# QK-norm attention and a squared-ReLU feed-forward on one core: output weights loaded in parts, odd pairs' squares in a free weight form, a scale and the last rows moved

## The chip, the cores and the metric

The kernel runs on one core of a Trainium2 chip. The time is the device time of one execution in microseconds (us). Three executions of the kernel before took 1393.12, 1393.48 and 1394.81 us; the median is 1393.48.

The engines of a core work side by side, each on its own instructions in order: TensorE (PE in the profile, PEld for its weight loads), VectorE (DVE), ScalarE (ACT), GpSimd (POOL) and SyncE (SP), which issues nearly all DMAs here. They wait for each other on semaphores.

## The reference

Attention over 8 batches, 12 heads, 448 positions and 64 channels, with q and k divided by their root mean square and multiplied by a gain; then a feed-forward with a squared ReLU on the 3584 tokens of 768 channels.

```python
def rmsnorm(x, g):
    rms = np.sqrt(np.mean(x * x, axis=-1, keepdims=True) + 1e-06)
    return x / rms * g
q_n, k_n = (rmsnorm(q, g_q), rmsnorm(k, g_k))
scores = scale * np.matmul(q_n, k_n.transpose(0, 1, 3, 2))
scores = scores - np.max(scores, axis=-1, keepdims=True)
attn = np.exp(scores)
attn = attn / (np.sum(attn, axis=-1, keepdims=True) + 1e-09)
x = np.matmul(attn, v)      # (B,H,S,D) -> (B*S, H*D)
h = np.maximum(x @ w_in, 0.0)
out = h * h @ w_out
```

Everything is float32.

## The kernel before

**Attention.** It goes by pairs of heads: 6 pairs to a batch, 48 in all, numbered i. Of each pair q and k are squared (`Rows.square`, L181, on ScalarE, into a tile `squares`), summed over channels by VectorE (`Rows.add`, L194 and L197), raised to the power -1/2 by GpSimd (`Rows.power`, L204), and q is scaled (`Rows.scale`, L219). From the third batch on q goes out to DRAM and comes back in blocks (`store_q`, `load_blocks`), VectorE transposes the blocks (`turn_blocks`, L367), and ScalarE multiplies the turned q by the gain (L369). The scores are matmuls (`score`, L435, L446), the exponentials ScalarE activations that write the tile `wT` (`weigh`, L454), the products with v matmuls (`attend`, L536, L550, L571), and the sums of the weights are added up by GpSimd (L473) and summed over partitions by matmuls with ones (L602, L611). `take_sums` puts them into a tile `inverse`, which `invert` or `invert_both` turns into reciprocals and GpSimd multiplies onto the result (L630 for an even pair, L690 for an odd one). `inverse` and `squares` are two names for one buffer: both have the tag "squares" with `bufs=1`, so each waits until the other has been used up. An even pair's squares have 512 columns, an odd one's 384, since the last 64 rows of two pairs are kept with the even one.

**Feed-forward.** It goes by units u of two batches, four units in all. The matrix products use fewer multiplications than the plain ones: products P1 to P7 of sums and differences of quarter blocks, in the first unit one level of it (L986), in units 1 to 3 two levels for the product with w_in (`deep_products`, L1042). Each unit has four blocks. In a block 28 steps of the deep products fill the tiles `hid`, then the generator `second_products` multiplies them by w_out (L1251, 384 columns each; one product of the source is 4 MATMULs in the trace). The output weights stand in DRAM as 8 forms of 128 x 384 ("11", "12", "21", "22", "T1" to "T4", in this order); a tile `out_sb` holds the 8 forms, two such tiles make a block, and there are two buffers for them. P1 reads form 11, P2 21, P3 22, P4 T4, P5 T1, P6 T2 and P7 T3. Form 12 is read only where the 64 last rows of a batch are multiplied (`multiply_rest`, L1165), which is in units 0 and 3; units 1 and 2 (`KEPT`) put those rows by in DRAM, and the last unit works them off as a row block `NT` of its own (`extra`).

**The order.** The source lays down each engine's order by hand. `run` steps the feed-forward's generators and after each step calls `follow_loads`, which counts down `later` (closures with a number of steps to wait), then takes some tasks of the attention: `tasks` and `pool_tasks`, the deques into which `prepare`, `additions` and the visits put their closures. A visit to a pair stands between the steps: its matmuls are one run on TensorE. `drain` ends a unit: it takes the rest of the stream and then all tasks. `visit_whole` is the visit to a pair from i = 25 on; it attends to pair i - 1 and scores pair i in turns.

The loads of the next output weights are put by at the end of a block (L902 issues them):

```python
later.append([4, lambda: [load_out(n + 2) for n in ns]])
```

Pieces of the deep weights (`load_piece`, L892) go into a ring `in_sb` of 42 places, some four pieces ahead of their use. All of these loads, and those of q, k and v, are in SP's one queue in the order of the source. The results of a row block are added up in `accs` by VectorE (L1345, L1272) or written first by ScalarE (L1341, L1266), and stored in the last block (`store`, L1350).

Of the kernel before, what the change touches and what calls it, by code (L numbers as in the profile page):

```python
# [14 lines left out]
F32 = mybir.dt.float32  # L15
# [8 lines left out]
P = 128  # L24
# [201 lines left out]
def program(ctx, tc, rows, v, g, wide, ones, moe_w_in, moe_w_out, out, shift):  # L226
# [50 lines left out]
    def whole(i):  # L277
        return i > 2 * 2 * NPAIR
# [85 lines left out]
    def turn_blocks(i, x):  # L364
        ensure("blocks", i, x)
        dst = att.tile([P, S], F32, name="qT" if x == 0 else "kT")
        nc.vector.transpose(dst, room_for_blocks(i, x))  # L367
        if x == 0:
            nc.scalar.mul(dst, dst, g)  # L369
        turned[i, x] = dst  # L370

    def load_v(i):
        b, c = pairs[i]
# [321 lines left out]

    def leave(i):
        b, c = pairs[i]
        for x in range(2):
            del turned[i, x]
        del values[i]  # L700
        if b == 1:
            begin_forms(c)
        elif b > 1:
            settle(b, c)
# [191 lines left out]
        side, place = divmod((n * 10 + PLACES[m]) % (2 * SIDE_OF_RING), SIDE_OF_RING)  # L896
        return ring[side][:, place]

    def load_out(n):
        if NF // 2 <= n < B // 2 * NF // 2:  # L900
            out_sb[n] = new_out()
            nc.sync.dma_start(out_sb[n], out_forms[n % (NF // 2)])  # L902

    roles = [banks[n] for n in (7, 6, 5)]

    def turn_roles(*order):
# [9 lines left out]
    FIRST_ORDER = ["P1", "P5", "P2", "P6", "P3", "P4", "P7"]  # L916
    FIRST_OF_BLOCK = ["P1", "rest0", "P5", "P4", "P6", "P2", "rest1", "P3", "P7"]
    SECOND_ORDER = ["P1", "P2", "P5", "P6", "P4", "P3", "P7"]
    SPLIT_ORDER = [
# [285 lines left out]
    def second_products(u, blk, hid, sums_, accs):  # L1205
# [20 lines left out]
                yield len(some) * COST_OUT  # L1226
            turn_roles(2, 1, 0)

        def store_rows(tt, e):
# [5 lines left out]
            store(accs[-1] if tt is None else accs_of(tt)[e], parts)  # L1235

        def accs_of(tt):
            return extra["accs"] if tt == NT else accs[2 * tt : 2 * tt + 2]
# [53 lines left out]
        if split:  # L1292
            places = [*roles, banks[1], banks[2]]
            for name, tt, n in SPLIT_ORDER:
# [9 lines left out]
                if tt:  # L1304
                    store_some(name)
                yield COST_OUT
        for tt in range(0 if split else NT + final):
            order = SECOND_ORDER if tt or not u else FIRST_OF_BLOCK
            for name in order:
                if name.startswith("rest"):  # L1310
                    a = int(name[-1])
                    multiply_rest(
                        u, blk, hid, banks[2:0:-1], PARTS_BY_ROW[2 * a : 2 * a + 2],
                        accs[-1] if a else None,
                    )
# [5 lines left out]
                product(tt, name, ps, nc.scalar if order is SECOND_ORDER else nc.vector)  # L1321
                if name == "P1" and order is FIRST_OF_BLOCK:
                    yield from sums_behind_first()
                    continue
                if order is not FIRST_OF_BLOCK:
                    store_some(name)
                yield COST_OUT
            turn_roles(2, 0, 1)
        while to_store and blk == NBLK - 1:
            some = to_store.popleft()  # L1330
            if final:
                store_rows(*some)
            else:
                later.append([2, lambda some=some: store_rows(*some)])
        for n in ns:
            del out_sb[n]
        later.append([4, lambda: [load_out(n + 2) for n in ns]])

    def add_to(acc, ps, first=False, engine=nc.scalar):
        if first and engine is nc.scalar:  # L1340
# [2 lines left out]
            nc.vector.tensor_copy(out=acc, in_=ps)  # L1343
        else:
            nc.vector.tensor_tensor(out=acc, in0=acc, in1=ps, op=ALU.add)  # L1345
    def store(acc, parts):

        at = 0
        for b, row, n in parts:
            nc.sync.dma_start(out[ds(b * S + row, n), :], acc[at : at + n, :])  # L1350
            at += n


# [181 lines left out]
    def follow_loads():  # L1535

        for some in to_load:
            some[0] -= 1
        while to_load and to_load[0][0] <= 0:
            load_weights(to_load.popleft()[1])  # L1540
        for some in later:
            some[0] -= 1
        while later and later[0][0] <= 0:
            later.popleft()[1]()

# [106 lines left out]
    def square(i, x, room, engine=None):  # L1652
        if i <= last:
            ensure("qk", i)
            ensure("qk", i - i % 2)
            rows.square(i, x, room[:, 0 : 4 * P], engine)

    def normalize(i, x):

# [67 lines left out]
    def visit_among(i, n):  # L1727
# [21 lines left out]
        elif whole(i + 1):  # L1749
            prepare(i + 3)  # L1750

    def prepare(i, gaps=0):

        if i > last:
            return
        room = []
        tasks.extend([gap] * gaps)
        tasks.append(
            lambda: room.append(io.tile([P, 4 * P], F32, name="squares", tag="squares", bufs=1))
        )  # L1760
# [11 lines left out]
    def visit_whole(i):  # L1772
        late = [some for some in tasks if getattr(some, "args", None) == (i,)]
        for some in late:
            tasks.remove(some)
        run_all()
        if shift:
            attend_all(i - 1)
            if i <= last:
                weigh_slots(i, 1)  # L1780
        else:
            if i % 2 == 0:
                both_denominators(i - 2)
            for n in range(NJ):
                attend(i - 1, (n,))
                forget(i - 1, (n,))
                if i <= last:
                    score(i, n)
                    weigh(i, n)
                while n == 1 and i % 2 == 0 and late:  # L1790
                    late.pop(0)()
            if i % 2:
                attend(i - 1, (NJ,))
                forget(i - 1, (NJ,))
            join_halves(i - 1)
            if i % 2 == 0:
                tasks.append(lambda: invert_both(i - 2))
                if i <= last:
                    score(i, NJ)
                    weigh(i, NJ)  # L1800
            if i <= last:
                additions(i)
        tasks.extendleft(reversed(late))
# [15 lines left out]
    with tc.manual_schedule(engines=ENGINES):  # L1819
# [8 lines left out]
        for i in range(len(pairs) + 1):  # L1828
            for n in range(1 if whole(i) else VISITS):
                at = i * VISITS + n - VISITS - unit  # L1830
                if at < 0:
                    visit_alone(i, n)
                    continue
                u, x = divmod(at, unit)
                if x == 0:
                    u, x = u - 1, unit
                run(place(u, x - (1 if whole(i - 1) else 0.5)))
                if i < last:
                    if whole(i) and not shift:
# [58 lines left out]
```

## Time and profile before

| what | value |
|---|---|
| median of three runs | 1393.48 us |
| the profiled execution | 1394.38 us |
| its span (first to last instruction of the program) | 1392.6 us |
| granted TensorE clock, mean | 0.998 |
| output weight loads | 24 of 1536 KB, 9.9 us to landing (6.6 to 12.9) |
| deep weight loads of 384 KB | 64, 4.2 us to landing |
| odd pairs' squares, one | 0.52 us |
| scale of a turned q, one | 0.67 us |
| last matmul ends, span ends | 1385.1, 1392.6 us |

The profile has one execution. "Busy" is the time in which an engine works, as a share of the span; an instruction that waits isn't counted. A line of the timeline has the start and the length in us, the engine, the source line, the operation, what it writes and reads, its shape and the number of instructions merged; in brackets stands how long the engine was idle before and for what. A line of the windows view has for each stretch the time of PE, PEld, DVE, ACT and POOL with instruction counts, then the granted TensorE clock, the DMA share and GB/s. Unit 0 of the feed-forward runs from about 128 to 487 us, unit 1 from 496 to 806, unit 2 to 1102, unit 3 to the end; attention goes on beside them until 1087 us.

### The profile page before, as it was taken

The numbers are of one execution on the slowest core, as the hardware profiler recorded it, in microseconds if no ns is written. First come the engines' busy times: TensorE is split into PE (matmuls) and PEld (weight loads), VectorE is DVE, ScalarE is ACT, GpSimd is POOL, SyncE is SP. The second block draws the span as 40 slices with busy tenths as digits, with TensorE's granted clock in tenths as the row PEclk, the third lists the DMA queues.
The fourth block names the chain that finished last, engine by engine and source line by source line (L and its number), as shares of the span: only waits on it lengthen the run. The fifth ranks groups of instructions, "written<-read, shape, count | busy, mean of one in ns | idle before, by whom it ended". The sixth has DMA issues, their size and how long they took to land.

```text
span 1392.6 us, 19474 instructions
## 1 busy us (share of the span) xinstructions
PE 1363.3 (98%) x6320; PEld 845.7 (61%) x6320; DVE 807.2 (58%) x1635; ACT 608.3 (44%) x1118; POOL 789.6 (57%) x794
## 2 busy tenths in 40 slices
PE   7999999999999999999999999999999999999997
PEld 3333444444444466676758586676768677868684
DVE  4786545867758755555556755455546642445444
ACT  6885477757666244353434244442434032202020
POOL 5668664746656868576667877566745630303030
PEclk9999999999999999999999999999999999999999
DMA  5566746968769875664739475755527442424223
GB/s 147 149 168 169 203 117 159 264 179 219 233 155 284 231 215 162 187 173 141 204 86 279 140 225 149 211 153 176 146 86 239 142 165 103 135 90 149 78 90 100
DMA packets 385588, 233.36 MB, mean 168 GB/s; under 512 B 272452, under 2 KB 354244, under 8 KB 381380
## 3 DMA queue, kind: packets, MB, share of 16 engines
q1 hardware_dynamic: 385184, 231.95, 57.7%
q8 instruction: 52, 0.85, 0.3%
q14 instruction: 60, 0.49, 0.1%
q10 hardware_dynamic: 292, 0.07, 0.0%
HBM read 174.59 MB, written 57.34 MB: 167 GB/s over the span
## 4 chain that ended last, share of the span: by engine, by line
PE 81%; POOL 4%; DVE 4%; DMA 3%; issue 3%; SPq 2%; ACT 2%; POOLq 0%; ACTq 0%; DVEq 0%
PE bank L1251 30%; PE bank L1042 20%; PE bank L986 8%; PE bank L446 5%; PE bank L536 5%; PE bank L550 4%; PE bank L435 4%; PE bank L1165 2%; POOL sum L473 2%; PE bank L585 1%; DMA qk<-in_k_dram 1%; PE bank L611 1%; SPq L326 1%; SPq L318 1%; PE bank L571 1%
## 5 line engine op out<-in xcount | busy, mean ns | idle before, releaser
L1042 PE MATMUL bank<-xT,in_sb 128*128 128x224 f32 x1344 | 289.3, 354 | 2.9 <-ACT part L1031 2.3
L1251 PE MATMUL bank<-out_sb,hid 128*128 128x384 f32 x768 | 272.5, 488 | 2.2 <-POOL out_sb L1514 1.4
L1345 DVE TENSOR_TENSOR acc<-acc,bank 128x384 f32<-128x384 f32 x312 | 166.6, 548 | 164.6 <-PE bank L1251 138.1
L1042 PEld LDWEIGHTS bank<-xT,in_sb 128*128 128x128 f32 x1344 | 252.6, 190 | 15.0 <-ACT wT L454 5.6
L454 ACT ACTIVATE wT<-bank,rr 128x448 f32<-128x448 f32 x288 | 163.5, 631 | 155.1 <-PE bank L435 92.7
L1251 PE MATMUL bank<-out_sb,sums 128*128 128x384 f32 x576 | 207.2, 490 | 1.3 <-DVE acc L1345 0.9
L1251 PEld LDWEIGHTS bank<-out_sb,hid 128*128 128x128 f32 x768 | 144.7, 190 | 104.5 <-issue 5.6
L204 POOL TENSOR_TENSOR rr<-ms,minus_half 128x8 f32<-128x8 f32 (+1 forms) x96 | 146.0, 1521 | 73.7 <-DVE ms L197 63.8
L1251 PEld LDWEIGHTS bank<-out_sb,sums 128*128 128x128 f32 x576 | 107.7, 190 | 86.3 <-issue 4.3
L1027 DVE TENSOR_TENSOR hid<-hid,bank 128x224 f32<-128x224 f32 x312 | 111.0, 383 | 83.9 <-PE bank L1042 79.1
L986 PE MATMUL bank<-xT,in_sb 128*128 128x448 f32 x336 | 131.9, 546 | 0.1
L473 POOL TENSOR_TENSOR sum<-sum,wT 128x448 f32<-128x448 f32 (+1 forms) x96 | 110.6, 1173 | 8.1 <-ACT wT L454 6.6
L986 PEld LDWEIGHTS bank<-xT,in_sb 128*128 128x128 f32 x336 | 62.1, 190 | 69.0 <-issue 60.2
L446 PE MATMUL bank<-qT,kT 64*128 64x448 f32 (+1 forms) x492 | 100.5, 571 | 1.9 <-DVE qT L409 1.1
L473 POOL TENSOR_TENSOR sum<-wT 128x448 f32<-128x448 f32 x48 | 55.8, 1183 | 69.8 <-ACT wT L454 69.8
L1099 ACT ACTIVATE hid<-hid 128x448 f32<-128x448 f32 x96 | 55.0, 573 | 66.7 <-DVE hid L1027 48.5
L435 PE MATMUL bank<-qT,kT 64*64 64x448 f32 x552 | 77.0, 547 | 1.9 <-ACT wT L454 1.9
L1042 PE MATMUL bank<-more,in_sb 128*128 128x224 f32 x288 | 76.2, 357 | 1.4 <-DVE hid L1037 1.4
L550 PE MATMUL bank<-wT,vt 64*64 64x448 f32 x576 | 74.3, 548 | 0.0
L1039 ACT COPY hid<-bank 128x448 f32<-128x448 f32 x24 | 12.8, 532 | 137.3 <-PE bank L1042 137.3
L369 ACT ACTIVATE qT<-qT,g 128x448 f32<-128x448 f32 x34 | 22.6, 665 | 113.7 <-DVE qT L367 113.7
L446 PEld LDWEIGHTS bank<-qT,kT 64*128 64x128 f32 (+1 forms) x492 | 34.9, 166 | 60.4 <-issue 36.8
(140 smaller groups left out, 2059.1 us busy)
## 6 DMA issues: line engine op xcount, KB each, us to landing
out_sb<-out_forms SPq DMA_DIRECT2D x24, 1536.0 KB, 9.9
in_sb<-in_deep SPq DMA_DIRECT2D x64, 384.0 KB, 4.2
in_sb<-in_deep SPq DMA_DIRECT2D x80, 256.0 KB, 4.1
words<-in_moe_w_in_dram SPq DMA_DIRECT2D x32, 384.0 KB, 3.8
words<-in_moe_w_out_dram SPq DMA_DIRECT2D x32, 384.0 KB, 3.6
out_forms<-out_sb SPq DMA_DIRECT2D x8, 1536.0 KB, 7.5
qk<-in_q_dram SPq DMA_DIRECT2D x96, 96.0 KB, 2.6
qk<-in_k_dram SPq DMA_DIRECT2D x96, 96.0 KB, 2.7
```

Of the source, the lines that this page charges most:

```text
L204: self.nc.gpsimd.tensor_tensor(out=self.rr[i][:, x, 0 : self.count(i)], in0=ms, in1=self.minus_half.to_broadcast(list(ms.shape)), op=ALU.pow,)
L435: nc.tensor.matmul(sc[ds(half * D, D)], lhsT=turned[i, 1][ds(e * D, D), ds(m * P + half * D, D)], rhs=turned[i, 0][ds(e * D, D), :], start ...
L446: nc.tensor.matmul(sc[some], lhsT=turned[p, 1][r, keys], rhs=turned[p, 0][r, :], start=True, stop=True,)
L454: nc.scalar.activation(new_weights((i, m), e), sc, AF.Exp, scale=rows.rr[i][:, 1, 2 * m + e : 2 * m + e + 1],)
L473: nc.gpsimd.tensor_tensor(out=sums[i, e][some], in0=left[some], in1=weights[key_of(i, m), e][some], op=ALU.add)
L536: nc.tensor.matmul(values_bank(i)[ds(e * D, D), :], lhsT=lasts[i % 2][mine, e, :] if m == NJ else values[i][:, m, e, :], rhs=weights[key_o ...
L550: nc.tensor.matmul(bank[ds(e * D, D), :], lhsT=values[i][keys, n, e, :], rhs=weights[(i, n), e][keys], start=n == 0, stop=n == NJ - 1 and ...
L986: nc.tensor.matmul(ps, lhsT=w_sb[:, IN.index(left), c, :], rhs=forms[u, c][right], start=first and c == 0, stop=c == NK - 1, skip_group_ch ...
L1027: nc.vector.tensor_tensor(out=quarter(name, n), in0=quarter(base, n), in1=ps, op=ALU.add)
L1042: nc.tensor.matmul(ps, lhsT=left, rhs=right, start=start, stop=stop, skip_group_check=True)
L1251: nc.tensor.matmul(ps, lhsT=extra[left][:, t] if tt == NT else lefts[left][:, t, ts(tt, P)], rhs=w_sb[t][:, OUT.index(right), :], start=fi ...
L1345: nc.vector.tensor_tensor(out=acc, in0=acc, in1=ps, op=ALU.add)
```

## The change

It has four parts.

1. The loads of the output weights of units 1 to 3 go in parts: four slices of two forms for each of the two tiles, 4, 7, 10 and so on up to 25 steps after the end of the block before. The order is forms 11 and 12, then T3 and T4, T1 and T2, 21 and 22. In units 1 and 2 form 12 is left out.
2. An odd pair's squares go into the place of form 12 of the lower of the output weight tiles at hand, if it is of unit 1 or 2. Even pairs' squares, and those outside these units, stay with the tag "squares".
3. While `drain` closes a unit ahead of a whole visit, the scale of the turned q is put by and issued at the end of `visit_whole`, or before the pair is left. The lists of instructions show it for one pair, at i = 25.
4. In the last unit the row block of the kept rests (`NT`) comes second instead of last. In the last block's last row block P7 comes before P3, the first half of the columns of one store goes out behind P2, and the other half at the end.

TensorE, VectorE, ScalarE and GpSimd have as many instructions as before; SP has 1323 DMAs in place of 1250.

```diff
         nc.vector.transpose(dst, room_for_blocks(i, x))
+        turned[i, x] = dst
         if x == 0:
+            to_scale.append(dst)
+            if not closing:
+                scale_turned()
+
+    def scale_turned():
+        while to_scale:
+            dst = to_scale.popleft()
             nc.scalar.mul(dst, dst, g)
-        turned[i, x] = dst
...
-    def load_out(n):
-        if NF // 2 <= n < B // 2 * NF // 2:
+    def load_out(ns):
+
+        unit_of = ns[0] * 2 // NF
+        if not 0 < unit_of < B // 2:
+            return
+        for k, some in enumerate((ds(0, 1 if unit_of in KEPT else 2), ds(6, 2), ds(4, 2), ds(2, 2))):
+            for t, n in enumerate(ns):
+                forms_to_load.append([4 + 3 * (2 * k + t), partial(load_forms, n, some)])
+
+    def load_forms(n, some):
+        if n not in out_sb:
             out_sb[n] = new_out()
-            nc.sync.dma_start(out_sb[n], out_forms[n % (NF // 2)])
+        nc.sync.dma_start(out_sb[n][:, some], out_forms[n % (NF // 2)][:, some])
...
+    LAST_ORDER = ["P1", "P2", "P5", "P6", "P4", "P7", "P3"]
...
-        for tt in range(0 if split else NT + final):
-            order = SECOND_ORDER if tt or not u else FIRST_OF_BLOCK
+        for tt in () if split else (0, NT, 1, 2) if final else range(NT):
+            ends = final and blk == NBLK - 1 and tt == NT - 1
+            order = LAST_ORDER if ends else SECOND_ORDER if tt or not u else FIRST_OF_BLOCK
...
+                if ends and name == "P2":
+                    store_rows(tt, 0, slice(0, HALF))
...
             if final:
-                store_rows(*some)
+                store_rows(*some, slice(0 if some[1] else HALF, DM))
...
-        later.append([4, lambda: [load_out(n + 2) for n in ns]])
+        load_out([n + 2 for n in ns])
...
+        for some in forms_to_load:
+            some[0] -= 1
+        while forms_to_load and forms_to_load[0][0] <= 0:
+            forms_to_load.popleft()[1]()
...
-            rows.square(i, x, room[:, 0 : 4 * P], engine)
+            rows.square(i, x, room[:, 0 : (3 if i % 2 else 4) * P], engine)
...
+    def room_for_squares(i):
+
+        n = min(out_sb, default=0)
+        if i % 2 and n * 2 // NF in KEPT and n * 2 // NF > 0 and 3 * P <= HALF:
+            return out_sb[n][:, OUT.index("12")]
+        return io.tile([P, 4 * P], F32, name="squares", tag="squares", bufs=1)
...
-            lambda: room.append(io.tile([P, 4 * P], F32, name="squares", tag="squares", bufs=1))
+            lambda: room.append(room_for_squares(i))
...
+        closing = False
+        scale_turned()
         tasks.extendleft(reversed(late))
...
                 if x == unit:
+                    closing = whole(i)
                     drain()
```

More of the change, by code (lines that the diff above doesn't have):

```diff
@@ L367, in turn_blocks @@
         nc.vector.transpose(dst, room_for_blocks(i, x))
+        turned[i, x] = dst
         if x == 0:
+            to_scale.append(dst)
[4 more added lines that the diff above has]
+            dst = to_scale.popleft()
             nc.scalar.mul(dst, dst, g)
-        turned[i, x] = dst
+    to_scale, closing = deque(), False
     def load_v(i):
@@ L897, in form_of @@
         return ring[side][:, place]
-    def load_out(n):
-        if NF // 2 <= n < B // 2 * NF // 2:
+    def load_out(ns):
[7 more added lines that the diff above has]
+        if n not in out_sb:
             out_sb[n] = new_out()
-            nc.sync.dma_start(out_sb[n], out_forms[n % (NF // 2)])
+        nc.sync.dma_start(out_sb[n][:, some], out_forms[n % (NF // 2)][:, some])
+    forms_to_load = deque()
     roles = [banks[n] for n in (7, 6, 5)]
@@ L1227, in second_products, with store_rows @@
             turn_roles(2, 1, 0)
-        def store_rows(tt, e):
+        def store_rows(tt, e, columns=slice(None)):
             if tt is None or tt == NT:
@@ L1234, in store_rows @@
                 parts = [(2 * u + e, REST * e + P * tt, P)]
-            store(accs[-1] if tt is None else accs_of(tt)[e], parts)
+            store(accs[-1] if tt is None else accs_of(tt)[e], parts, columns)
         def accs_of(tt):
@@ L1320, in second_products @@
                 ps = roles[PRODUCTS[name][0]][:, 0:HALF]
-                product(tt, name, ps, nc.scalar if order is SECOND_ORDER else nc.vector)
+                product(tt, name, ps, nc.vector if order is FIRST_OF_BLOCK else nc.scalar)
                 if name == "P1" and order is FIRST_OF_BLOCK:
@@ L1345, in add_to, with store @@
             nc.vector.tensor_tensor(out=acc, in0=acc, in1=ps, op=ALU.add)
-    def store(acc, parts):
+    def store(acc, parts, columns=slice(None)):
         at = 0
         for b, row, n in parts:
-            nc.sync.dma_start(out[ds(b * S + row, n), :], acc[at : at + n, :])
+            nc.sync.dma_start(out[ds(b * S + row, n), columns], acc[at : at + n, columns])
             at += n
@@ L1772, in visit_whole @@
     def visit_whole(i):
+        nonlocal closing
         late = [some for some in tasks if getattr(some, "args", None) == (i,)]
@@ L1802, in visit_whole @@
                 additions(i)
+        closing = False
+        scale_turned()
         tasks.extendleft(reversed(late))
```

## The prediction

> **What bounds the kernel now.** I read the engine shares of the page first, then the tail of the timeline, then who TensorE waits for, and last what stands ahead of those waits on ScalarE.
>
> ```profile
> PE 1363.3 (98%) x6320; PEld 845.7 (61%) x6320; DVE 807.2 (58%) x1635; ACT 608.3 (44%) x1118; POOL 789.6 (57%) x794
> 1140.00:1385.00 245.00, 245.00 (x950) 179.24 (x948) 108.17 (x222) 44.15 (x89) 48.77 (x50) 1.00 0.29 103
> 1385.00:1393.00 8.00, 0.07 (x1) 0.00 (x0) 1.02 (x2) 0.00 (x0) 0.00 (x0) 0.81 0.42 104
> ```
>
> TensorE (PE) is the bound: 1363.3 of 1392.6 us. In the last unit (1140 to 1385 us) it is busy without a break, so nothing there but the 7.5 us after the last matmul can be won. The other 22 us of idle time lie before 1080. The change adds no matmul, so it can win idle time, badly paced stretches and the tail. In 500 to 1080 us TensorE waits for this:
>
> ```profile
> PE bank L1042 <- ACT part L1031: 2.3, 4, 0.6
> PE bank L1042 <- DVE hid L1027: 1.5, 3, 0.8
> PE bank L1042 <- DVE hid L1037: 1.4, 3, 0.5
> PE bank L1251 <- DVE acc L1345: 0.6, 1, 0.6
> PE bank L1042 <- DMA in_sb<-in_deep: 0.6, 1, 0.6
> PE bank L1251 <- ACT acc L1341: 0.4, 2, 0.2
> ```
>
> The columns are total us, times, longest. The sum is 6.8 us. What holds ScalarE (ACT) up is in its own list for 500 to 1000 us and in the timeline around one of the four L1031 waits:
>
> ```profile
> ACT squares L181 <- POOL xT L690: 31.2, 8, 11.8
> ...
> 526.19 1.14 POOL L690 TENSOR_TENSOR xT<-xT,inverse 128x448 f32<-128x448 f32 x1
> 527.36 0.52 ACT L181 ACTIVATE squares<-qk 128x384 f32<-128x384 f32 x1 [3.30 <-POOL xT L690]
> 527.79 0.33 ACT L1031 COPY part<-bank 128x224 f32<-128x224 f32 x1
> 528.17 1.81 PEld L1042 LDWEIGHTS bank<-xT,in_sb 128*128 128x128 f32 x10 [0.86 <-ACT part L1031]
> ```
>
> The squares of an odd pair (128x384) wait 3.30 us for GpSimd's last use of `inverse`, since both tiles share one buffer; a bank copy stands behind the squares on ScalarE, and TensorE wants that bank. The same happens on the scale of qT:
>
> ```profile
> 490.20 0.67 ACT L369 ACTIVATE qT<-qT,g 128x448 f32<-128x448 f32 x1 [6.06 <-DVE qT L367]
> 490.77 2.44 ACT L454 ACTIVATE wT<-bank,rr 128x448 f32<-128x448 f32 x4
> 491.44 0.59 PE L435 MATMUL bank<-qT,kT 64*64 64x448 f32 x2 [1.89 <-ACT wT L454]
> ...
> 492.00:494.00 2.00, 2.00 (x20) 0.83 (x16) 0.00 (x0) 1.07 (x2) 2.00 (x3) 0.55 0.26 59
> 494.00:496.00 2.00, 2.00 (x14) 0.52 (x8) 0.00 (x0) 1.03 (x2) 1.92 (x3) 0.60 0.60 100
> ```
>
> The reader should see that the 1.89 us of idle time is not all: the third value from the end in the last two lines is the granted clock, 0.55 and 0.60 just after the wait, and 1.00 elsewhere.
>
> [...]in 499 to 520 us, behind the two 1536 KB loads (11.7 us to landing), 56 KB loads took 9.8 us. [...]the 384 KB stores in 1366 to 1380 us landed after 2.3 us.
>
> **The change part by part.**
>
> *Odd squares in form 12's place.* No instruction is added; the instruction lists of the two programs show all 20 odd squares of the units that keep their rests writing `out_sb` now, with no wait for GpSimd. The 31.2 us of waits on ScalarE go. What TensorE gets of it: the four waits for L1031 (0.52 at 528.17, 0.59 at 682.94, 0.61 at 837.85, 0.61 at 991.80, sum 2.3) each follow such a square by under 1.2 us; the three for L1037 (0.49, 0.40, 0.51, sum 1.4) follow the squares of 582.79, 736.15 and 891.64, where VectorE's sum L194 stood waiting for the square ahead of L1037. The 0.64 at 797.45 follows a VectorE subtraction of 2.24 us as well, so I count half, 0.3. I take 4.0; the bounds are 2.3 (only L1031) and 4.4 (all). The 1.5 us on L1027 stand behind even squares, which stay where they are: unchanged. VectorE's L194 merely moves earlier, beside other work.
>
> *The scale at the unit's end.* One ACTIVATE L369 of 0.67 us moves behind six exponentials L454 and two copies. Its wait of 6.06 us for VectorE's transpose (done at 490.16) then ends before ScalarE arrives. The price is read from the visit as a whole: from 486.33 to the next feed-forward matmul at 496.29 it takes 9.96 us for 24 + 24 + 8 matmuls; the same 56 take 5.61 us at 588.50 (to 594.11). The difference, 4.35 us, is 1.89 idle, about 1.7 of half clock (3.4 us at 0.5) and the rest pacing by ScalarE. I take 4.2; the bounds are 1.9 (the idle alone, if the pace stays) and 4.4. The moved scale is needed one visit later, at about 509 us, so it is hidden.
>
> *The end.* Row block 2 is last instead of the kept rests, and P3 comes after P7. Before: last matmul, two VectorE adds to 1386.13, then two 64-row stores issued at 1386.16 and 1386.67 (landing 3.2 to 4.0 us). After: P7's adds and its 128-row store lie beside P3's four matmuls (1.29 us); behind P3 stand one add (0.56) and one 128-row half-width store. Counting from the same last matmul: add 1385.11 to 1385.67, issue at 1385.7 against 1386.67 (1.0 saved), landing after 2.3 against 3.6 (1.3 saved): 2.3, and I take 2.2. The bounds are 1.0 (landing no shorter) and 2.6. The half store of the upper columns, one more DMA, is behind P2 and hidden. The kept rests move 18 us earlier within a stretch where TensorE never waits: nothing.
>
> *Loads in parts.* 24 loads of 1536 KB become 96, 72 more issues of 0.43 us on SyncE's queue (31 us over 880 us), and 16 of them leave out 192 KB. Gain: in block 0 of unit 1 the SP queue was stuck behind the loads, and TensorE's wait of 0.57 at 532.32 for `in_sb` should shrink; I take 0.4, bounds -0.5 and 0.6. Loss: the last part (forms 21 and 22) goes out three steps before the second products begin. It is needed at product 7, P2, whose second half reads it. A product is 4 MATMULs here, 1.29 us. The tightest is block 3 of unit 1:
>
> ```profile
> 764.17 1.46 PE L1251 MATMUL bank<-out_sb,hid 128*128 128x384 f32 x4
> ...
> 764.52 1.61 SPq L326 DMA_DIRECT2D q_rows<-qk  x3
> 766.23 1.96 SPq L892 DMA_DIRECT2D in_sb<-in_deep  x4
> ```
>
> The new issue stands between these two SP lines, at 766.1. The second product starts at 766.21 (two deep matmul groups lie between), P2 five products later at 772.66 and its second half at 773.3: 7.2 us of room. Five more parts ahead in the queue cost 2.2 us, and a 384 KB load lands in about 4.2 (the page's `in_sb` row): 0.8 us left. The other blocks have 9 us or more. I take 0.3 lost, bounds 0 and 3. What is queued behind each part on SP are pieces for the deep ring, four pieces ahead of use, and q, k, v of a later pair: covered while SP keeps up.
>
> *Sum.* 4.0 + 4.2 + 2.2 + 0.4 - 0.3 = 10.5 us. The profiled execution took 1394.38 (span 1392.6 and 1.8 around it), 0.9 above the median of 1393.48, and the parts are differences, so I take them from the median: 1383.0.
>
> **Rivals.**
>
> A, the sum: 1383.0. For it: each wait taken away has its follower on TensorE in the timeline. Against: small waits may reappear one instruction later.
>
> B, half of it: the visit at 486 keeps its slow pace (1.9 only), the squares give only the four L1031 waits (2.3), the end gives 2.2: 6.4, so 1387.1. For it: VectorE and GpSimd are busy 57 to 58% and may be late themselves.
>
> C, hardly anything: the waits move to VectorE or the queue, the end gives 1.5, late parts take some: 1391.5.
>
> D, slower: SP falls behind. SP issues nearly without pause in 743 to 771 us; with six more parts a block its lag carries over from block to block, and last parts land late at P2. It decides from 7.2 us after issue in block 3, from 9 elsewhere. If landing came 12 us after issue (the 1536 KB loads took 6.6 to 12.9), each of 8 blocks would stall about 2.5 us, 20 in all, less 10.5: 1403. Against: bytes fall, and the large loads, behind which SP stood blocked (one issue of 4.46 us at 505.73), go.
>
> **How the numbers follow.** Chances: A 0.62, B 0.24, C 0.07, D 0.07. The forecast is A's 1383.0. Its own bounds, 12.5 and 7 won, give 1381 to 1386.5; B's low end, 1.9 + 2.3 + 1.0 - 1, gives 1389. The range is 1380.8 to 1389.3. A difference of 0.2% (2.8 us) is about what a measurement of this kernel tells from no change: faster by more is A and B, 0.86; within is C, 0.07; slower is D, 0.07.
>
> **What would show it.** In the changed profile: no wait of ScalarE's squares for L690; the L1031 and L1037 waits of TensorE gone; the visit before 500 us taking 5.7 us with the clock at 1.00; span end about 5.3 us after the last matmul instead of 7.5. Wrong would be: TensorE waiting for `out_sb<-out_forms` at L1251, a half-clock stretch anywhere in the body, or ScalarE's wait moved to the loads of qk.

## The result and the profile after

The changed kernel takes 1381.67 us (median of four runs, 1381.07 to 1382.63) against 1393.48. The ratio is 0.9911, with a 95% interval of 0.9899 to 0.9922. The forecast was 1383.0, within a range of 1380.8 to 1389.3. The profiled execution took 1381.76 us, its span is 1379.6 (before 1392.6).

The first view is the engine shares on the page of the changed kernel.

```profile
PE 1358.1 (98%) x6320; PEld 847.1 (61%) x6320; DVE 807.7 (59%) x1635; ACT 608.0 (44%) x1118; POOL 789.8 (57%) x794
```

All instruction counts are the same, and TensorE still sets the time. Its busy time fell by 5.2 us although it has the same 6320 matmuls: that part of the gain was never idle time. It was matmuls stretched by a halved clock (0.50 for 3.4 us at the visit of 487 us in the kernel before, from 492.18 to 495.60), or badly paced (behind the wait at 528.17 us, for one, three starts 0.247 to 0.302 us apart where one comes every 0.189).

The next view is who TensorE waits for in 500 to 1080 us (total us, times, longest).

```profile
PE bank L1064 <- DVE hid L1049: 1.4, 3, 0.7
PE bank L1273 <- DVE acc L1370: 0.6, 1, 0.6
PE bank L1273 <- ACT acc L1366: 0.4, 2, 0.2
```

L1064 is the deep product that was L1042, L1049 was L1027, L1053 was L1031, L1059 was L1037; L1273 is the second product (L1251). The four waits for ScalarE's copy, the three for VectorE's L1037 and the one for `in_sb` are gone; the three behind even squares (1.5, now 1.4) and the one for `acc` at 797 us (now at 789.57) are as they were. The timeline at the first pair of odd squares, the place that the prediction shows for 526 to 528 us, tells why.

```profile
520.58 0.53 ACT L181 ACTIVATE out_sb<-qk 128x384 f32<-128x384 f32 x1
522.43 0.35 ACT L1053 COPY part<-bank 128x224 f32<-128x224 f32 x1 [1.31 <-PE bank L1064]
...
522.83 1.14 POOL L699 TENSOR_TENSOR xT<-xT,inverse 128x448 f32<-128x448 f32 x1
...
524.07 0.52 ACT L181 ACTIVATE out_sb<-qk 128x384 f32<-128x384 f32 x1 [0.21 <-DVE ms L194]
```

The squares write `out_sb`. The first (520.58) starts without a wait, 2.3 us before GpSimd's multiplication (522.83), on which it waited 3.30 us before. The copy that stood behind it on ScalarE (522.43) now waits for nothing but its own matmul. The second square (524.07) waits 0.21 us for VectorE. In ScalarE's own list of waits for 500 to 1000 us the wait for L690 (L699 here) is gone; a part of it has moved to VectorE, since a pair's second squares are written over its first, which VectorE must have summed:

```profile
ACT out_sb L181 <- DVE ms L194: 17.4, 10, 12.3
```

The visit at 487 us has this timeline and these windows (the third value from the end is the granted clock).

```profile
489.35 1.21 PE L444 MATMUL bank<-qT,kT 64*64 64x448 f32 x8
...
490.32 1.16 ACT L463 ACTIVATE wT<-bank,rr 128x448 f32<-128x448 f32 x2 [0.26 <-PE bank L444]
490.85 1.21 PE L444 MATMUL bank<-qT,kT 64*64 64x448 f32 x8
...
493.76 0.70 ACT L377 ACTIVATE qT<-qT,g 128x448 f32<-128x448 f32 x1
```

```profile
488.00:490.00 2.00, 2.00 (x26) 0.87 (x19) 1.90 (x6) 1.10 (x2) 2.00 (x2) 1.00 0.79 177
490.00:492.00 2.00, 2.00 (x28) 1.30 (x22) 0.88 (x2) 1.33 (x4) 1.92 (x3) 1.00 0.09 20
```

The scale (now L377) runs behind the visit, the exponentials follow their matmuls at once, TensorE is never idle and the clock stays at 1.00. The visit's 56 matmuls take from 487.04 to 492.74, which is 5.70 us instead of 9.96.

The tail, in the timeline:

```profile
1373.95 1.16 SPq L1375 DMA_DIRECT2D out_dram<-acc  x2
1374.19 0.55 DVE L1370 TENSOR_TENSOR acc<-acc,bank 128x384 f32<-128x384 f32 x1 [0.27 <-PE bank L1273]
```

One add stands behind the last matmul, and the second of the two stores goes out at 1374.78. The span ends 5.43 us after the last matmul's end (1374.16), before 7.5.

The two programs run the same matmuls in the same order up to the last unit, so the start of the k-th matmul of one can be set against that of the k-th of the other. This gives where the 13.0 us between the two spans came from, with the forecast beside it:

| place | forecast, us | from matched matmuls, us |
|---|---|---|
| before the visit (470 us, VectorE's `acc`) | 0 | -0.72 |
| visit at 487 us | 4.2 | 4.27 |
| behind seven odd squares | 3.7 | 7.13 |
| `acc` wait at 797 us | 0.3 | 0 |
| wait for `in_sb` at 532 us | 0.4 | 0.80 |
| a late last part (765 us) | -0.3 | -0.24 |
| small drifts elsewhere | 0 | -0.33 |
| after the last matmul | 2.2 | 2.07 |
| sum | 10.5 | 13.0 |

The -0.72 at 470 us is mostly a wait for `acc` that grew from 0.25 to 0.85 us; of the profiles below only one has such a wait there (0.53 us), so it scatters from execution to execution. The late part landed at 765.21, 0.14 us ahead of the matmul that reads it; the 0.24 us that this cost are too little for the list of waits.

### The profile page after: what moved, and what is told of

It reads as the page before. It is cut to its first block, busy times and chain, and to the rows that moved or that the text cites. A ratio compares the mean times of both kernels' runs of the same rounds, so it can differ in the third digit from the quotient of the medians.

```text
span 1379.6 us, 19591 instructions
## 1 busy us (share of the span) xinstructions
PE 1358.1 (98%) x6320; PEld 847.1 (61%) x6320; DVE 807.7 (59%) x1635; ACT 608.0 (44%) x1118; POOL 789.8 (57%) x794
## 4 chain that ended last, share of the span: by engine, by line
PE 88%; DVE 3%; DMA 2%; ACT 2%; SPq 2%; POOL 2%; issue 1%; POOLq 0%; DVEq 0%; ACTq 0%
PE bank L1273 31%; PE bank L1064 25%; PE bank L1008 8%; PE bank L455 5%; PE bank L545 5%; PE bank L559 4%; PE bank L444 4%; PE bank L1187 2%; PE bank L594 1%; DMA qk<-in_k_dram 1%; PE bank L620 1%; PE bank L611 1%; PE bank L580 1%; DVE acc L1370 1%; PE bank L410 1%
## 5 line engine op out<-in xcount | busy, mean ns | idle before, releaser
L1064 PE MATMUL bank<-xT,in_sb 128*128 128x224 f32 x1344 | 288.0, 353 | 0.0
L1273 PE MATMUL bank<-out_sb,hid 128*128 128x384 f32 x768 | 273.3, 488 | 2.4 <-POOL out_sb L1539 1.4
L1064 PEld LDWEIGHTS bank<-xT,in_sb 128*128 128x128 f32 x1344 | 253.0, 190 | 10.4 <-ACT wT L463 5.6
L1273 PEld LDWEIGHTS bank<-out_sb,hid 128*128 128x128 f32 x768 | 144.9, 190 | 104.7 <-issue 6.2
L1273 PE MATMUL bank<-out_sb,sums 128*128 128x384 f32 x576 | 207.1, 490 | 1.9 <-DVE acc L1370 1.5
L1273 PEld LDWEIGHTS bank<-out_sb,sums 128*128 128x128 f32 x576 | 107.8, 190 | 86.8 <-DVE acc L1370 5.3
L1049 DVE TENSOR_TENSOR hid<-hid,bank 128x224 f32<-128x224 f32 x312 | 111.4, 384 | 83.1 <-PE bank L1064 78.1
L1117 POOL TENSOR_TENSOR hid<-hid 128x448 f32<-128x448 f32 x24 | 27.2, 1141 | 123.1 <-DVE hid L1049 118.7
L1064 PE MATMUL bank<-more,in_sb 128*128 128x224 f32 x288 | 74.3, 353 | 0.0
```

What stands on the lines that cost most here:

```text
L1049: nc.vector.tensor_tensor(out=quarter(name, n), in0=quarter(base, n), in1=ps, op=ALU.add)
L1064: nc.tensor.matmul(ps, lhsT=left, rhs=right, start=start, stop=stop, skip_group_check=True)
L1273: nc.tensor.matmul(ps, lhsT=extra[left][:, t] if tt == NT else lefts[left][:, t, ts(tt, P)], rhs=w_sb[t][:, OUT.index(right), :], start=fi ...
```

## The experiments

Eleven kernels were run. The first four undo one part of the change each; the next three apply one part to the kernel before; then come a pair of parts, and three variants. Where loads go "in one go" below, it is still without form 12 in units 1 and 2: 192 and 1152 KB for each tile instead of 1536. The kernel before was timed again beside each group of runs; its medians are 1393.48 (with the change), 1394.31, 1393.57, 1393.72 and 1393.25 us. A difference of two medians from different groups is therefore good to about 1 us.

**The squares undone.**

```diff
-        if i % 2 and n * 2 // NF in KEPT and n * 2 // NF > 0 and 3 * P <= HALF:
+        if False:
             return out_sb[n][:, OUT.index("12")]
```

> The changed kernel with the odd pairs' squares back in the shared buffer, all else as changed. Theory 1 (each part pays at its own place on TensorE): comparing each matmul's start in the profiles before and after, the steps that follow an odd square add up to 7.0 us, so this kernel should be about 7.0 us slower than the changed one, 1388.6, with TensorE's waits for L1053 and L1059 (the bank copies and sums behind the squares) back, seven in all. Theory 2 (the gain in these units is mostly the relief of the DMA queues by loads in parts): under 3 us slower, at most 1384.5. Theory 3 (the squares give what the profile shows as idle time only, 3.7 us): 1385.4.

Measured: 1388.19 us (1387.77 to 1389.91), ratio to the kernel before 0.9961 (0.9947 to 0.9976): 6.5 us more than with the squares moved. TensorE's waits for 500 to 1080 us in this kernel:

```profile
PE bank L1064 <- ACT part L1053: 2.4, 4, 0.6
PE bank L1064 <- DVE hid L1049: 1.5, 3, 0.8
PE bank L1064 <- DVE hid L1059: 1.4, 3, 0.5
```

The seven waits that the moved squares had removed are back, 2.4 + 1.4 = 3.8 us by this list, and undoing the part costs 6.5 (6.8 by matched matmuls from 500 us on, against the changed kernel). The list shows too little, and the matched matmuls show why. At 528.17 in the kernel before, the list has 0.52 us. A matmul of 224 columns there has a record of 0.353 us, but one starts every 0.189, so idle time begins to count 0.164 us late: start to start the wait was 0.867, which is 0.68 lost. The next matmul starts 0.294 after, another 0.10. Some ten matmuls on come three starts 0.247, 0.302 and 0.294 apart, 0.28 together, and here the records still overlap, so that the list has nothing at all. The sum is 1.06 where the list has 0.52.

**The scale undone.**

```diff
-                    closing = whole(i)
+                    closing = False
```

> The changed kernel with the scale of the turned q issued at once again. Theory 1: the visit at 486 us takes 9.9 us again in place of 5.7, with some 1.9 us idle and a stretch of 3.4 us at half clock; 4.2 us slower than the changed kernel, 1385.9. Rival (the half clock belongs to the place, not to the idle time, or another wait comes): 1.9 us slower or less, 1383.6. The later visits shouldn't change.

Measured: 1385.56 us (four runs, 1383.32 to 1386.9), ratio 0.9941 (0.9924 to 0.9958): 3.9 more. The profiled run was the one of 1383.32, with a mean clock of 1.0; the other three have 0.998 or 0.999. Its timeline and windows at the visit:

```profile
490.09 0.67 ACT L377 ACTIVATE qT<-qT,g 128x448 f32<-128x448 f32 x1 [6.07 <-DVE qT L367]
...
491.33 0.59 PE L444 MATMUL bank<-qT,kT 64*64 64x448 f32 x2 [1.90 <-ACT wT L463]
```

```profile
490.00:492.00 2.00, 0.67 (x8) 0.44 (x12) 0.06 (x1) 1.91 (x4) 2.00 (x3) 1.00 0.27 81
492.00:494.00 2.00, 2.00 (x22) 0.74 (x16) 0.00 (x0) 1.68 (x4) 2.00 (x3) 1.00 0.23 44
```

The same 1.90 us of idle time is there as in the kernel before (1.89), but here no half clock follows: the visit takes 8.28 us (486.21 to 494.49), 2.58 more than in the changed kernel, not 4.26. So the wait has a sure price of some 2.6 us and a second part, 1.7, that only some executions pay. Two more profiles below have the scale at its old place: with the loads alone the visit takes 9.96 us with 3.4 us at half clock, with the squares alone 8.28 without. In these four profiles the idle times are 1.89 to 1.91 us, and half clock stands behind two of them (0.50 for 3.4 us in the kernel before, too). What decides between the two outcomes was not shown.

**The loads undone.**

```diff
-        for k, some in enumerate((ds(0, 1 if unit_of in KEPT else 2), ds(6, 2), ds(4, 2), ds(2, 2))):
-            for t, n in enumerate(ns):
-                forms_to_load.append([4 + 3 * (2 * k + t), partial(load_forms, n, some)])
+        for n in ns:
+            for some in (ds(0, 1), ds(2, 6)) if unit_of in KEPT else (ds(0, 8),):
+                forms_to_load.append([4, partial(load_forms, n, some)])
```

> The changed kernel with the output weights loaded in one go again, 4 steps after the block before (form 12 still left out in units 1 and 2, where the squares stand). Theory 1: only the wait for the deep weights in the first block of unit 1 comes back (0.75 us) and the 0.3 us lost at 765 and 794 go, so 0.5 us slower, 1382.2, within the noise of the times. Theory 2 (the queues' relief is worth more): 3 us slower or more, 1384.7 and up, with TensorE waiting for in_sb, or SP far behind in units 1 and 2.

Measured: 1388.57 us (1386.5 to 1391.26), ratio 0.9955 (0.9938 to 0.9971). The part to which the forecast gave 0.1 us net is worth 6.9 here. The profiled run was the slowest of the four, 1391.26 us, so its waits are longer than the median's. TensorE's waits in 500 to 1080 us begin with a new row:

```profile
PE bank L1064 <- DMA in_sb<-in_deep: 6.6, 2, 5.4
```

The 5.4 us are at 533 us, and the windows around it show what it draws after it:

```profile
528.00:530.00 2.00, 0.00 (x0) 0.00 (x0) 0.00 (x0) 1.94 (x5) 1.23 (x2) 1.00 0.49 110
...
534.00:536.00 2.00, 2.00 (x7) 1.82 (x6) 0.05 (x1) 0.00 (x0) 0.51 (x1) 0.50 1.00 365
536.00:538.00 2.00, 2.00 (x4) 1.05 (x4) 0.63 (x2) 0.00 (x0) 0.00 (x0) 0.50 1.01 392
```

TensorE stands still, then runs at half speed. (The second wait, 1.2 us at 842 us, is in unit 2.) SP's timeline gives the reason (L921 loads output weights, L902 deep weights):

```profile
500.83 2.75 SPq L921 DMA_DIRECT2D out_sb<-out_forms  x4
...
505.14 6.73 SPq L326 DMA_DIRECT2D qk<-in_k_dram  x4
511.97 3.51 SPq L326 DMA_DIRECT2D qk<-in_q_dram  x2
...
529.03 2.44 SPq L902 DMA_DIRECT2D in_sb<-in_deep  x5
```

and that of the changed kernel the contrast:

```profile
502.85 1.95 SPq L326 DMA_DIRECT2D qk<-in_k_dram  x4
504.89 2.11 SPq L326 DMA_DIRECT2D qk<-in_q_dram  x2
...
521.08 1.01 SPq L902 DMA_DIRECT2D in_sb<-in_deep  x2
```

Behind the large loads SP takes 6.73 us to issue four small ones, 4.04 of it for one of them (with parts 1.95 for all four), and the deep weights that TensorE wants at 527 to 528 go out at 529.03 instead of 521.08. The DMA engines are fully busy from 502 to 512 us in both kernels (DMA share 0.95 to 1.12 here, 0.93 to 1.05 in the changed one), which points to the order of the transfers and not to their sum. The kernel before has the lag, too:

```profile
503.98 6.98 SPq L326 DMA_DIRECT2D qk<-in_k_dram  x4
...
527.92 2.43 SPq L892 DMA_DIRECT2D in_sb<-in_deep  x5
```

It cost 0.57 us there, because TensorE itself came to this place some 5 us later.

**The end undone.**

```diff
-        for tt in () if split else (0, NT, 1, 2) if final else range(NT):
-            ends = final and blk == NBLK - 1 and tt == NT - 1
+        for tt in () if split else range(NT + final):
+            ends = False
...
-                store_rows(*some, slice(0 if some[1] else HALF, DM))
+                store_rows(*some)
```

> The changed kernel with the last unit's row blocks and the last stores in the old order. Theory 1: 2.1 us slower, 1383.8, all of it behind the last matmul: 7.5 us from its end to the span's end in place of 5.4. Rival (the tail is set by something else, such as the end of the program, and the earlier row block NT moved the rest): no difference in the tail, under 1 us.

Measured: 1384.24 us (1383.61 to 1385.64), ratio 0.9932 (0.9915 to 0.9948): 2.6 more. The last matmul ends at 1374.02, as with the change; the tail is 7.69 us instead of 5.43. Four 64-row stores go out again:

```profile
1373.36 3.75 SPq L1375 DMA_DIRECT2D out_dram<-qk  x4
1374.06 1.02 DVE L1370 TENSOR_TENSOR qk<-qk,bank 128x384 f32<-128x384 f32 x2 [0.73 <-PE bank L1273]
```

The tail scatters, but the two orders don't mix: in the six profiles with the old end it takes 7.50 to 9.50 us, in the seven with the new one 5.40 to 6.52 (six of them up to 5.68).

The four parts, each undone by itself, cost 6.5 + 3.9 + 6.9 + 2.6 = 19.9 us (by the ratios 7.0, 4.2, 6.1 and 2.9), but the whole change brought 11.8. They aren't independent: the loads' 6.9 can't be a gain of their own. The theory from here on: the deep weights at 532 us are a deadline that SP sets; whatever brings TensorE there sooner runs into it, unless the loads are cut up.

**The scale alone, on the kernel before** (the edits of the squares, the loads and the end undone together).

> The kernel before with the deferred scale alone (the output weights still in one go, though without form 12 in units 1 and 2). Theory 1, refined: in the first block of unit 1 the deep weights arrive at a moment that the SP queue sets, about 532 us, whenever TensorE gets there; so the 4.2 us won at 486 us come back as a longer wait for in_sb, 0.6 + 4.2 = about 5 us, perhaps with half clock behind it, and the time is 1393 to 1395, no gain. Rival (the parts add up, and the loads' loss in the run without parts came from the squares): 1389.3.

Measured: 1395.10 us (1393.63 to 1398.97) against 1393.57 before, ratio 1.0012 (1.0005 to 1.0019). No gain, as theory 1 said. The visit is 4.3 us shorter, and 3.3 of it is given back at one place: in the profile of this kernel TensorE waits

```profile
PE bank L1064 <- DMA in_sb<-in_deep: 2.1, 1, 2.1
```

and the windows behind that wait are at half clock:

```profile
528.00:530.00 2.00, 0.68 (x4) 0.71 (x5) 0.00 (x0) 1.94 (x5) 1.04 (x2) 1.00 0.90 298
530.00:532.00 2.00, 2.00 (x7) 1.36 (x6) 0.69 (x2) 0.76 (x2) 1.93 (x3) 0.60 1.01 369
532.00:534.00 2.00, 2.00 (x6) 1.36 (x5) 0.55 (x1) 0.00 (x0) 1.77 (x2) 0.55 1.03 401
```

The wait is 2.1 us where about 5 was expected; the half clock behind it takes 1.7 more. The last matmul still ends 1.1 us sooner than in the kernel before. What makes this profile longer is its tail, 9.50 us instead of 7.50, so the 1.5 us lost in the medians aren't explained in full. The loads stand here as two transfers for each tile instead of one; what that does by itself was not tried.

**The loads in parts alone** (squares, scale and end undone).

> The kernel before with the loads in parts alone (form 12 left out in units 1 and 2, squares and scale as before, the end as before). Theory 1, refined: the wait for in_sb at 532 us goes (0.75 us), the visit at 486 us and the squares' waits stay: about 1393.0, no change that can be measured. Rival (parts of loads are worth the 6.9 us that their removal cost, whatever else is done): 1387.

Measured: 1393.65 us (1390.47 to 1394.35), ratio 1.0000 (0.9991 to 1.0009). The wait for `in_sb` is gone, which brings 0.8 us at that place in the profile, but in the time nothing of it shows (by the interval it is under 1.3 us): cutting up the loads earns next to nothing while the visit of 486 us is slow.

**The squares alone** (scale, loads and end undone).

> The kernel before with the odd squares in form 12's place alone (the output weights in one go without form 12, scale and end as before). Theory 1, refined: of the seven waits behind odd squares, the first (1.1 us, at 528 us) turns into a longer wait for in_sb 4 us later, the other six (5.9 us) are won: 1387.6, or a little less if the loads come late in unit 2 too (1.2 us were lost at 842 us when loads came in one go with everything else changed). Rival (all of it needs the loads in parts): 1392 or more.

Measured: 1388.13 us (1386.78 to 1390.7), ratio 0.9963 (0.9951 to 0.9976), so 5.4 us of gain. Its profile shows five of the seven gains whole, at 0.9 to 1.1 us. Of the first, 0.5 us is given back at the wait of 1.10 us behind it (529 us), and of the fifth only 0.2 is left (a wait of 0.62 at 835 us, in unit 2):

```profile
PE bank L1064 <- DMA in_sb<-in_deep: 1.7, 2, 1.1
```

**Scale and loads together** (squares and end undone).

> The kernel before with the deferred scale and the loads in parts, and neither the moved squares nor the changed end. The scale alone took 1395.1 and the parts alone 1393.65, so added up they give about 1395. Theory 1 (a deadline): the scale's gain of some 4 us in the visit was given back at 529 us because the deep weights came late behind the whole loads; with the loads in parts they come in time, so the gain stays: about 1389.3, with no wait of TensorE for in_sb near 530 us. Theory 2 (the two parts are independent of each other, and the 6.9 us that the parts were worth in company belong to the moved squares): about 1394 to 1395. A result of 1391 to 1392 would say that half of it does.

Measured: 1390.49 us (1388.57 to 1392.19) against 1393.72, ratio 0.9978 (0.9970 to 0.9986). One part lost 1.5, the other nothing; together they gain 3.2, and the waits for 500 to 1080 us have no row for `in_sb`:

```profile
PE bank L1064 <- ACT part L1053: 2.4, 4, 0.6
PE bank L1064 <- DVE hid L1049: 1.5, 3, 0.8
PE bank L1064 <- DVE hid L1059: 1.5, 3, 0.5
```

This is theory 1's sign, and its time but for 1.2 us; in the profiled run, one of 1389.78, the matmul at 532 us comes 4.9 us sooner than before, and no half clock follows. Independence (1394 to 1395) is out. With this run the parts add up in one order: before 1393.7; scale and loads, 1390.5; the squares, 1384.2 (the run with the end undone); the end, 1381.7. That is 3.2, 6.3 and 2.6.

**Loads in one go, later.** Is it the cutting that helps, or only that the loads don't stand ahead of the first deep weights of unit 1?

```diff
+            forms_to_load.append([4, partial(load_forms, n, None)])
+        for n in ns:
             for some in (ds(0, 1), ds(2, 6)) if unit_of in KEPT else (ds(0, 8),):
-                forms_to_load.append([4, partial(load_forms, n, some)])
+                forms_to_load.append([18, partial(load_forms, n, some)])
```

(The first line only takes the tile, so that the squares still find form 12's place.)

> The changed kernel with the loads of a block in one go (four transfers of 192 and 1152 KB, form 12 left out in units 1 and 2) but issued 18 steps after the end of the block before instead of 4. It tells whether it is the cutting up of the loads or the moment of the large ones that counts. Theory 1 (moment: only the first steps of unit 1 have no slack for the deep weights, since there the four pieces ahead are fetched from nothing): no wait near 532, 1382 to 1383. Theory 2 (cutting: a large load delays the deep pieces behind it wherever it stands): the wait for in_sb comes again, some 15 to 20 us later in unit 1's first block and perhaps in others, and 3 to 7 us of the 6.9 stay lost, 1385 to 1389.

Measured: 1398.94 us (1397.34 to 1401.08), ratio 1.0038 (1.0024 to 1.0052): outside of both. TensorE's waits from 500 us to the end of the last unit begin with

```profile
PE bank L1276 <- DMA out_sb<-out_forms: 11.6, 8, 2.9
```

There is no row for `in_sb`, as theory 1 said, but now the output weights themselves are late. Most of it is in unit 3, where each tile is one load of 1536 KB and waits of 2.95, 2.93 and 2.50 us stand at 1127, 1201 and 1277 us. With the last two come 6.8 and 3.4 us of half clock, with the first none. (All lines of this kernel and the next stand three further down than those of the changed kernel.) Both theories had left that side out.

**In between**, at step 11 (the same edit with 11 for 18):

> As the run with whole loads at step 18, but at step 11. At step 4 the large loads made the deep weights late (in_sb, 6.6 us with the half clock), at step 18 they were late themselves (out_sb, in unit 3 above all). Theory 1 (it is only the moment, and cutting up is one way among others): at step 11 neither wait comes, 1382 to 1384. Theory 2 (the large loads leave no moment that is free, since they hold the queue for some 10 us and the pieces ahead cover about as much; cutting is what helps): waits of 1 us or more for in_sb or out_sb stay in unit 1 or unit 3, 1385 to 1390.

Measured: 1389.08 us (1386.88 to 1393.22), ratio 0.9972 (0.9964 to 0.9980), in theory 2's range. The loads now stand at another place in SP's queue, and the deep weights behind them are late again:

```profile
509.43 2.01 SPq L924 DMA_DIRECT2D out_sb<-out_forms  x4
...
514.48 3.79 SPq L326 DMA_DIRECT2D q_rows<-qk  x3
522.47 1.90 SPq L326 DMA_DIRECT2D qk<-q_rows  x4
...
526.90 2.44 SPq L902 DMA_DIRECT2D in_sb<-in_deep  x5
```

This time the lag is made by the round trip of q through DRAM: the three `q_rows` stores land up to 7.8 us after issue (3.0 in the changed kernel), and SP, which loads them back, stands until 522.47, with the deep weights queued behind. At 531.38 TensorE has been idle for 4.68 us. The trace puts this down to a sum of GpSimd, which ended at about the same time; but the piece of deep weights that went out at 527.54 landed at 531.24, 0.14 us ahead of that matmul, and with the loads at step 4 the same piece landed 0.13 ahead of it (533.20 and 533.33). So I read it as the deep weights here too. A half-clock stretch of 6.8 us lies over that place, and waits for `in_sb` of 0.68 and 1.65 follow at 610 and 764 us. Of the three moments tried, none serves for whole loads; the parts do serve.

**One more gap for even squares.** The three L1049 waits that are left stand behind even squares; one more empty step ahead of the task that sums them might let them pass.

```diff
             if not first:
-                tasks.append(gap)
+                tasks.extend([gap] * (1 if i % 2 else 2))
```

> The changed kernel with the sum of an even pair's squares (L194) put one more step behind the squares. What is left of TensorE's waits in units 1 and 2 are three behind even squares (0.34, 0.70 and 0.36 us, some 1.9 us by the matmuls' starts), where VectorE has the sum ahead of the additions that free TensorE's banks. If the place of the sum is the cause, these go, 1.9 us in the profile and 1379.8 at best; if VectorE is late there anyway, they stay, or turn up one step later: 1381.7.

Measured: 1382.89 us (1382.43 to 1383.35), ratio 0.9924 (0.9908 to 0.9941), so no gain over 1381.67. The waits in 500 to 1080 us:

```profile
PE bank L1273 <- DVE acc L1370: 1.3, 2, 0.6
PE bank L1064 <- DVE hid L1049: 0.8, 1, 0.8
```

The three are gone and two new ones have come, at 778 and 808 us: VectorE's sum has only been moved into the way of something else. The last matmul ends at 1374.11, as with the change (1374.16); what this profile has more is in its tail (6.52 us instead of 5.43). Nothing tried here was faster than the change itself.

## Why the prediction was right, and which terms were mis-sized

The forecast named the places and the signs correctly, and its sum (10.5) met 11.8 measured. That they are so close is in part luck. The squares were priced 3 us too low, and a third of that was hidden by losses that scatter or that nobody forecast (-0.72 and -0.33 in the table). And the loads in parts, priced at next to nothing, happened to be the part without which the others lose 6.9 us. The two ends that the forecast gives its sum, 12.5 and 7 us won, are not the sums of its own bounds, which are 12.0 (4.4 + 4.4 + 2.6 + 0.6) and 1.7 (2.3 + 1.9 + 1.0 - 0.5 - 3). Step by step:

*Odd squares in form 12's place*: the mechanism was right, the term was mis-sized: 4.0 was said, with 4.4 as the upper bound, and what came is 6.5 by undoing it, 6.3 on top of scale and loads, 5.4 alone, and 7.1 by matched matmuls. The step priced each of seven waits at the idle time that the list displays, 0.40 to 0.61. That leaves out 0.16 us of overlap between the records, and the slower starts after each wait; each was worth 0.88 to 1.08. The 0.3 for the wait at 797.45 was wrong: it is VectorE's own lateness and stayed.

*The scale at the unit's end*: 4.2 was said, 4.27 found, 3.9 by undoing it. Taking the price from the visit as a whole instead of from the 1.89 us of idle time was what made it right. That 1.7 of it isn't paid in every execution was not foreseen. Nor was the condition: alone this part earns nothing, since most of what it gains is taken again at 529 to 532 us.

*Loads in parts*: said +0.4 and -0.3, found +0.80 and -0.24 by matched matmuls. The step looked at the wait of 0.57 us as it stood and priced it as if TensorE came to 532 us at the same time as before. With the steps above TensorE arrives some 5 us sooner, the 0.57 becomes 5.4 and a half-clock stretch (in the slowest run), and the part is worth 6.9 in that company, and nothing measurable without. The forecast of the whole was not hurt, since all parts came together. Rival D, SP falling behind, was close to the mechanism and had it the wrong way round: it is the whole loads that make SP late. What the prediction set against D, one issue of 4.46 us behind the large loads, was this very lag, but it was given no price.

*The end*: 2.2 said, 2.07 found (2.6 by undoing it), with two terms that cancel. The issue came 0.98 sooner after the last matmul (1.0 said). The landing was no shorter: the 128-row half store had 13 of its 16 completions after 2.0 us, but the last came at 3.83 (2.3 said, 1.3 saved). What made up for it is that the span ends 1.0 us after the last landing (1378.61) instead of 2.3 (1390.30). Of that, 0.92 us before lies between the last landing and SP's first closing wait to end; what holds it wasn't tried and stays open.

Of what was to show it: no wait of squares for GpSimd's multiplication in 500 to 1000 us, no L1031 or L1037 waits, a visit of 5.7 us at full clock and a tail of 5.4 all came in. None of the three signs of being wrong appeared, unless one counts the 0.24 us behind the late part at 765 us.

## What to carry to other kernels

Price a wait by the distance between starts around it, against the undisturbed spacing, and not by displayed idle time: with overlapping matmul records the idle time was little more than half of the cost (3.8 of 6.8 us with the squares undone). Ask of a gain what the bound engine meets when it arrives sooner: a small wait on a transfer behind the place can be a deadline that grows by what is gained ahead of it, as the one at 532 us did (0.57 us in the kernel before, 5.4 in the profile with the loads undone). A part that earns nothing by itself may be the one that lets the others count, so test parts by undoing them as well as by doing them alone.

## What was not expected of the hardware

The same idle stretch of 1.9 us on TensorE, at the same place of the program, was followed by half clock in two profiles (0.55 in the windows of the kernel before) and by full clock in two others, so a single profile can over- or understate such a wait by 1.7 us. Longer waits scatter, too: with the loads at step 18, one of 2.95 us stayed at full clock, and one of 2.93 came with 6.8 us of half clock.

Behind two tiles' loads in one go SP needed 6.73 us to issue four small loads that with parts take 1.95, although the DMA engines were as busy in both cases.

The last completion of a store can trail: the 384 KB store of 1373.95 had 14 of its 16 within 2.3 us and the last at 4.3 us, the half store behind it was alike (13 within 2.0 us, the last at 3.83). A 384 KB store 8 us earlier (1366.21) had landed whole in 2.34 us. A median of landing times says little about the end of a program.
